# Matmuls that read their moving columns from two halves by turns, in a gated FNet and SwiGLU kernel

## The chip, the cores and the metric

One core of a Trainium2 chip runs the kernel. The time is the device time in microseconds (us) of one execution. Before the change three runs took 709.20, 709.61 and 709.89 us, so the median is 709.61 us. The host transposes and stacks the inputs before the launch and the output after it; that work is not in the time.

## The reference

`x` is 2048 x 512 (sequence by hidden), all data float32. Cut to what matters:

```python
g = sigmoid((x * gate_w).sum(-1, keepdims=True))
a = dft_seq_re @ (x @ dft_hid_re.T) - dft_seq_im @ (x @ dft_hid_im.T)   # real part of a 2-D DFT
b = (silu(x @ w1) * (x @ w3)) @ w2                                       # F = 1376
return g * a + (1 - g) * b
```

## The kernel before, in words

**Layout.** Every product has the sequence position on the free axis: the output is stored as 512 x 2048 (hidden by sequence), and the host transposes it. The sequence is cut into four pieces of `TB = 512` columns, and a matmul on TensorE (PE) takes a 128 x 128 block of weights (the stationary operand) and 128 x 512 moving columns, one such piece, and adds to one PSUM bank of 128 x 512.

**Three matmuls for one.** A float32 number is split into a rounded high part (ScalarE, `high`, line 108) and the rest, a low part (VectorE, `low`, line 111). Both have the type float32r, 4 bytes an element. `mm3` (line 117) multiplies high by high, high by low and low by high, so a product of two blocks is three matmuls. All but the warm-up go through `mm3` (its matmul is line 119) or `half` (line 432), which does the same for the first chunk in another order.

**Seven products for eight.** Blocks are multiplied in a Strassen-like scheme: sums and differences of the four quadrants of each operand (forms such as `T1` to `T4`) give seven products, which are combined after them. VectorE makes the forms (lines 675 and 678 in `sum_c`), ScalarE and VectorE split them, and both read the products from PSUM.

**The stages.** Eleven bfloat16 matmuls on a constant (line 407, into `wps`) warm the engine. The gate stage runs over 21 items, a chunk of 128 hidden units of w1 and w3 with one half of the sequence each, in `gate_up`: x transposed (tile `xo`) is the moving operand, the weights are the stationary one (`wa`, `wb`), the products are X, Y and Z. One spare column of w1 carries `gate_w`, so the gate's score comes out with the last chunk and goes to `gs`. The result h goes to DRAM (`hsp`). Then come eight blocks, in `step`, whose products are called P and whose moving operand is always the tile `zo`:

- F, four blocks, one for each 512 positions: moving is a piece of the sequence DFT matrix (`cc`), stationary is x (`a`, forms A1 and A2). The result is multiplied by g (`gsp`) and goes to `zsp`.
- H, two blocks: moving is h from `hsp`, stationary is w2. The result is multiplied by 1 - g (`ngsp`) and goes to `nbsp`.
- Y, two blocks: moving is `zsp`, stationary is the hidden DFT matrix. The result plus the part in `nbsp` goes to `out`.

So the columns that F or the gate stage leave behind are moving columns once more in Y and H.

**What sets the order.** The order on every engine is written out by hand (`manual_schedule`). A step of the last eight blocks is 12 matmuls on one `zo` tile (6 in a few steps of H). Each step ends in `advance(m)`, which issues the load of what will be wanted 8 steps later (`LEAD + AHEAD`), makes the sums for 4 steps later and splits the `zo` tile for 3 steps later (`LEAD = 3`). There are four `zo` buffers.

**The gate's own work.** `gates` (lines 753 to 762) runs twice, once for each half of the sequence. For each of two pieces of 512 columns VectorE computes 1 - g from g (line 759) into `ng`; then ScalarE negates the second piece of `t` (line 760), and both tiles go to DRAM by GpSimd's queue. The blocks load from there, F from `gsp`, H from `ngsp` (`load_gate`).

Of the kernel before, what the change touches and what calls it, by code (L numbers as in the profile page):

```python
# [10 lines left out]
ALU = mybir.AluOpType  # L11

P = 128
S = 2048
D = 512
F = 1376
KD = D // P
TB = 512
NTB = S // TB
NT = TB // P  # L20
NST = S // P
NG = NST // 2
# [10 lines left out]
def fnet_swiglu_gate_kernel(  # L33
# [20 lines left out]
    nc = tc.nc  # L54
# [25 lines left out]
    def bank(k, name):  # L80
        return psum.tile([P, 512], F32, tag=f"ps{k}", name=name)
# [28 lines left out]
    def low(hi, lo, src):  # L110
        nc.vector.tensor_sub(lo, src, hi.bitcast(F32))  # L111

    def split(hi, lo, src):
        high(hi, src)
        low(hi, lo, src)

    def mm3(ps, ah, al, bh, bl, first, last, chain=False):
        for n, (u, v) in enumerate(((ah, bh), (ah, bl), (al, bh))):
            nc.tensor.matmul(ps, u, v, start=first and n == 0, stop=last and n == 2,  # L119
                             skip_group_check=chain)  # L120


    act0 = const.tile([P, 24], F32, tag="act0", name="act0")
# [139 lines left out]
    def prod(ps, n, wi, xi, start, chain=False):  # L263
        w = WSET[n]
        w, wi = (WA[w], wi) if wi < 3 else (WB[w], wi - 3)
        x = XO[ITEMS[n][1]]
        for q in range(2):
            sl = slice(q * P, (q + 1) * P)
            mm3(ps, w[:, 0, wi, sl], w[:, 1, wi, sl], x[:, 0, xi, q, :], x[:, 1, xi, q, :],
                start and q == 0, q == 1, chain)  # L270
# [148 lines left out]
    C = {(i, j): bank((0, 4, 6, 7)[2 * i + j], f"C{i}{j}") for i in range(2) for j in range(2)}  # L419

    def half(i, j, w, x, start):

        wp = lambda h, sl: a21[:, h, sl] if w is None else WA[0][:, h, w, sl]
        xp = lambda q, h: b12[:, h, q * 512 : (q + 1) * 512] if x is None else XO[0][:, h, x, q, :]
        hh, lh, hl = (0, 0), (1, 0), (0, 1)
        order = [(r, *p) for r in range(2) for p in ((hh, hl, lh) if w is None else (hh, lh, hl))]
        if w == x == 0:
            order = [(r, *p) for some in ((hh, lh), (hl,)) for r in range(2) for p in some]  # L430
        for n, (r, u, v) in enumerate(order):
            nc.tensor.matmul(C[i, j], wp(u, slice(r * P, (r + 1) * P)), xp(r, v),  # L432
                             start=start and n == 0, stop=not start and n == 5)

    def xo_half(k, q):
        i = OPS.index(k)
# [15 lines left out]
    split_by_both(*xo_half("B11", 0))  # L452
    split(*xo_half("B11", 1))
    half(0, 0, 0, 0, True)
    split(a21[:, 0], a21[:, 1], WS[0][:, 3])
    half(1, 0, None, 0, True)
    high(*wa_parts(0, 1, 3)[::2])
    low(*wa_parts(0, 1, 2))
    split_by_both(*xo_half("B21", 0))
    split(*xo_half("B21", 1))  # L460
    low(*wa_parts(0, 2, 3))
    half(0, 0, 1, 1, False)
    split(b12[:, 0], b12[:, 1], ST[0, "B12"])
    half(1, 0, 2, 1, False)
# [120 lines left out]
    for n in range(NI):  # L585
        if n in W2_AT:
            p = W2_AT.index(n)
# [4 lines left out]
        if n in A1_AT:  # L592
            p = A1_AT.index(n)
# [9 lines left out]
    n = NI - 1 - LOOK  # L603
# [149 lines left out]
    def gates(g):  # L753

        t, ng = GATES.pop(g)
        nc.scalar.activation(t, t, AF.Sigmoid)
        for j, (v, w) in enumerate(((-1.0, 1.0), (1.0, -1.0))):
            b = slice(j * 512, (j + 1) * 512)
            nc.vector.tensor_scalar(ng[:, b], t[:, b], v, w, op0=ALU.mult, op1=ALU.add)
        nc.scalar.activation(t[:, 512:], t[:, 512:], AF.Copy, scale=-1.0)  # L760
        nc.gpsimd.dma_start(gsp[g], t)
        nc.gpsimd.dma_start(ngsp[g], ng)
# [101 lines left out]
    def step(m):  # L864
# [19 lines left out]
        for r in range(2):  # L884
            sl = slice(r * P, (r + 1) * P)
            for n, zn in steps:
                for i in range(ni):
                    w = ws[2 * n + i]
                    b = slice(i * 512, (i + 1) * 512)
                    mm3(ps[r], w[:, 0, f, sl], w[:, 1, f, sl], zn[:, 0, b], zn[:, 1, b],  # L890
                        own and n == 0 and i == 0, n == NQ[blk] - 1 and i == ni - 1, not own)
# [55 lines left out]

    at(0, 0, lambda: nc.scalar.activation(act0, act0, AF.Sigmoid))
    at(0, 4, gates, 0)
    at(1, 3, gates, 1)  # L950
    late = [(w2, w2sp, p) for p in range(len(W2_AT), NP2)] + [(dd, dsp, p) for p in range(KD)]
    for i, (src, sp, p) in enumerate(late):
        blk, b = 1 + i // 2, i % 2
        n = (17, 24)[b]
# [84 lines left out]
```

## Time and profile before

| | |
|---|---|
| median of 3 runs | 709.61 us (709.20 to 709.89) |
| span of the profiled execution, first to last instruction | 707.2 us |
| TensorE matmul (PE) busy | 702.7 us, 99%, 3089 matmuls |
| TensorE weight load (PEld) busy | 579.2 us, 82% |
| VectorE (DVE) busy | 605.3 us, 86% |
| ScalarE (ACT) busy | 370.1 us, 52% |
| GpSimd (POOL) busy | 64.2 us, 9% |
| moved by DMA | 172.54 MB, mean 244 GB/s |

The time of the profiled execution is shown by its span alone; 2.4 us lie between the span and the median of the runs. PE busy means that a matmul is in the engine, by ends that are modelled, and matmuls overlap: one takes 389 ns from start to end, and the next starts well before that. The pace of the matmuls is therefore read as a stretch divided by the matmuls in it, not from the duration of one. PEld is the load of the next stationary block, which runs beside the matmul before it.

### The profile page before, as it was taken

What the parts mean: (1) busy time and instruction counts of PE and PEld (TensorE: products, weight loads), DVE (VectorE), ACT (ScalarE), POOL (GpSimd) and SP (SyncE); (2) the same over time, 40 slices, a digit from 0 to 9 for tenths busy, and PEclk for the clock granted to TensorE, in tenths of its full rate; (3) what the DMA queues carried; (4) which work ended last, traced back from release to release, by engine and by line L of the source; (5) the groups of instructions that cost most, each with busy time, mean ns of one, the idle gap of its engine ahead of it and who ended that gap; (6) DMA issues with size and microseconds to landing.
All of it is one profiled execution on the core that took longest, in us unless ns stands there. A gap on an engine that the chain in (4) does not pass through costs nothing.

```text
span 707.2 us, 8607 instructions
## 1 busy us (share of the span) xinstructions
PE 702.7 (99%) x3089; PEld 579.2 (82%) x3089; DVE 605.3 (86%) x737; ACT 370.1 (52%) x480; POOL 64.2 (9%) x118
## 2 busy tenths in 40 slices
PE   9999999999999999999999999999999999999997
PEld 6888888888888888888888888888888888888886
DVE  7989978887679999877999689969997896898985
ACT  6666555655446754454554454544555454455452
POOL 0011111211010000000110001100110000000000
PEclk9999999999999999999999999999999999999999
DMA  7665546589997566712595238914999971873932
GB/s 282 239 261 228 214 181 255 184 320 352 419 410 273 212 208 237 277 60 89 181 388 220 90 131 322 335 59 180 389 418 416 355 272 53 301 286 134 320 120 89
DMA packets 45547, 172.54 MB, mean 244 GB/s; under 512 B 5312, under 2 KB 5696, under 8 KB 41664
## 3 DMA queue, kind: packets, MB, share of 16 engines
q1 hardware_dynamic: 32608, 118.63, 45.7%
q0 software_dynamic: 12608, 52.97, 18.9%
q8 instruction: 24, 0.39, 0.2%
q10 hardware_dynamic: 288, 0.39, 0.2%
q14 instruction: 19, 0.16, 0.1%
HBM read 114.82 MB, written 57.16 MB: 243 GB/s over the span
## 4 chain that ended last, share of the span: by engine, by line
PE 99%; DVE 0%; ACT 0%; issue 0%
PE P L119 69%; PE X L119 16%; PE Z L119 8%; PE Y L119 4%; PE C L432 2%; PE wps L407 1%; DVE zc L829 0%; ACT zc L827 0%
## 5 line engine op out<-in xcount | busy, mean ns | idle before, releaser
L119 PE MATMUL P<-zo,a 128*128 128x512 f32 x1344 | 304.8, 389 | 0.0
L119 PEld LDWEIGHTS P<-zo,a 128*128 128x128 f32 x1344 | 252.3, 188 | 52.4
L108 ACT ACTIVATE zo<-B 128x1024 fp32r<-128x1024 f32 (+1 forms) x182 | 189.6, 1045 | 190.6 <-PE P L119 101.2
L111 DVE TENSOR_TENSOR zo<-B,zo 128x1024 fp32r<-128x1024 f32 (+1 forms) x182 | 218.0, 1204 | 48.7 <-ACT zo L108 48.2
L119 PE MATMUL P<-zo,H 128*128 128x512 f32 x468 | 106.2, 389 | 0.0
L119 PEld LDWEIGHTS P<-zo,H 128*128 128x128 f32 x468 | 87.8, 188 | 18.2
L675 DVE TENSOR_TENSOR B<-B,B 128x1024 f32<-128x1024 f32 (+1 forms) x78 | 92.9, 1191 | 0.1
L119 PE MATMUL X<-xo,wb 128*128 128x512 f32 x378 | 92.7, 389 | 0.0
L119 PEld LDWEIGHTS X<-xo,wb 128*128 128x128 f32 x378 | 70.9, 188 | 14.7
L119 PE MATMUL P<-zo,Y 128*128 128x512 f32 x336 | 76.3, 389 | 0.0
L119 PEld LDWEIGHTS P<-zo,Y 128*128 128x128 f32 x336 | 63.1, 188 | 13.1
L327 POOL DMA_DIRECT2D hsp<-h x42 | 23.1, 550 | 127.3 <-DVE h L381 76.1
L119 PE MATMUL X<-xo,wa 128*128 128x512 f32 x126 | 32.0, 389 | 0.0
L119 PE MATMUL Y<-xo,wa 128*128 128x512 f32 x126 | 32.0, 389 | 0.0
L119 PE MATMUL Z<-xo,wb 128*128 128x512 f32 x126 | 32.0, 389 | 0.0
L119 PE MATMUL Z<-xo,wa 128*128 128x512 f32 x126 | 32.0, 389 | 0.0
L678 DVE TENSOR_TENSOR B<-B,B 128x1024 f32<-128x1024 f32 x26 | 31.7, 1220 | 0.0
L904 ACT ACTIVATE zu<-P 128x512 f32<-128x512 f32 x32 | 19.1, 598 | 20.4 <-PE P L119 20.4
L375 DVE TENSOR_TENSOR u<-u,X 128x512 f32<-128x512 f32 x21 | 14.4, 688 | 16.8 <-PE X L119 16.8
L119 PEld LDWEIGHTS Y<-xo,wa 128*128 128x128 f32 x126 | 23.6, 188 | 4.9
L119 PEld LDWEIGHTS X<-xo,wa 128*128 128x128 f32 x126 | 23.6, 188 | 4.9
L119 PEld LDWEIGHTS Z<-xo,wb 128*128 128x128 f32 x126 | 23.6, 188 | 4.9
(137 smaller groups left out, 552.2 us busy)
## 6 DMA issues: line engine op xcount, KB each, us to landing
B<-cc SPq DMA_DIRECT2D x64, 512.0 KB, 6.3
hsp<-h POOLq DMA_DIRECT2D x42, 256.0 KB, 3.6
B<-hsp SPq DMA_DIRECT2D x20, 512.0 KB, 10.5
wbsp<-wb POOLq DMA_DIRECT2D x8, 1024.0 KB, 4.2
wb<-wbsp SPq DMA_DIRECT2D x8, 1024.0 KB, 7.5
B<-zsp SPq DMA_DIRECT2D x16, 512.0 KB, 8.4
H<-w2sp SPq DMA_DIRECT2D x6, 1024.0 KB, 9.2
ws<-w SPq DMA_DIRECT2D x11, 512.0 KB, 5.2
```

Of the source, the lines that this page charges most:

```text
L108: nc.scalar.activation(hi, src, AF.Copy)
L111: nc.vector.tensor_sub(lo, src, hi.bitcast(F32))
L119: nc.tensor.matmul(ps, u, v, start=first and n == 0, stop=last and n == 2, skip_group_check=chain)
L327: nc.gpsimd.dma_start(hsp[g, b + k, j // 2, :, j % 2 * 512 : (j % 2 + 1) * 512], h)
L375: nc.vector.tensor_add(u4, u4, x)
L407: nc.tensor.matmul(wps, warm[:, :P], warm, start=True, stop=True)
L432: nc.tensor.matmul(C[i, j], wp(u, slice(r * P, (r + 1) * P)), xp(r, v), start=start and n == 0, stop=not start and n == 5)
L675: nc.vector.tensor_add(t, t, RAW[blk, b, q][:, :n])
L678: nc.vector.tensor_sub(t, RAW[blk, "B12", q], t)
L904: nc.scalar.activation(U[name][:, r], ps[r], AF.Copy)
```

## The change

`mm3` and `half` no longer call the matmul directly, but through a helper that reads the 512 moving columns in another order: column 0 of the first half of 256, column 0 of the second half, column 1 of the first, column 1 of the second, and so on. In memory the two columns read one after the other lie 256 elements (1024 bytes) apart. What is written to PSUM is still 512 columns in a row.

So that the results are the same numbers, the host lays out the columns of x transposed and of the sequence DFT matrix in each piece of 512: the even ones first, then the odd ones. Read by turns they come out in their own order, and so the gate stage and F leave their columns in order. H and Y read such columns by turns, so that what they write is in turned order: position a * 256 + n of a piece is column 2n + a. For H's result the gate 1 - g has to be in the same order, and VectorE writes it so (every second element of `ng` from one half of `t`); the host undoes the order of the output. Numbers, sizes and order of the instructions on every engine stay as they were, as do all DMAs, their sizes and the patterns in which they read and write.

```diff
+    def turns(v):
+        return v.rearrange("p (a n) -> p n a", a=2)
+
+    def matmul(ps, u, v, **kw):
+        nc.tensor.matmul(ps.rearrange("p (n a) -> p n a", a=2), u, turns(v), **kw)
+
     def mm3(ps, ah, al, bh, bl, first, last, chain=False):
         for n, (u, v) in enumerate(((ah, bh), (ah, bl), (al, bh))):
-            nc.tensor.matmul(ps, u, v, start=first and n == 0, stop=last and n == 2,
-                             skip_group_check=chain)
+            matmul(ps, u, v, start=first and n == 0, stop=last and n == 2,
+                   skip_group_check=chain)
...
-            nc.tensor.matmul(C[i, j], wp(u, slice(r * P, (r + 1) * P)), xp(r, v),
-                             start=start and n == 0, stop=not start and n == 5)
+            matmul(C[i, j], wp(u, slice(r * P, (r + 1) * P)), xp(r, v),
+                   start=start and n == 0, stop=not start and n == 5)
...
-            nc.vector.tensor_scalar(ng[:, b], t[:, b], v, w, op0=ALU.mult, op1=ALU.add)
+            nc.vector.tensor_scalar(ng[:, b].rearrange("p (n a) -> p a n", a=2),
+                                    t[:, b].rearrange("p (a n) -> p a n", a=2),
+                                    v, w, op0=ALU.mult, op1=ALU.add)
...
+    def turns(v):
+        return v.reshape(*v.shape[:-1], TB // 2, 2).swapaxes(-1, -2).reshape(v.shape)
+
     cq = [
-        a[k].T.reshape(2, NG // 2, 2, P, NTB, TB).transpose(4, 0, 1, 3, 2, 5)
+        turns(a[k].T.reshape(2, NG // 2, 2, P, NTB, TB)).transpose(4, 0, 1, 3, 2, 5)
...
-    xq = x.T.reshape(2, 2, P, 2, 2, TB).transpose(3, 0, 4, 2, 1, 5)
+    xq = turns(x.T.reshape(2, 2, P, 2, 2, TB)).transpose(3, 0, 4, 2, 1, 5)
...
-    return np.ascontiguousarray(r.results[0]["out"].T).reshape(1, S, D)
+    y = r.results[0]["out"].reshape(D, NTB, TB // 2, 2).transpose(1, 3, 2, 0)
+    return np.ascontiguousarray(y).reshape(1, S, D)
```

## The prediction

> **What bounds the kernel now.** I read the page first: busy times, then the chain that ended last.
>
> ```profile
> PE 702.7 (99%) x3089; PEld 579.2 (82%) x3089; DVE 605.3 (86%) x737; ACT 370.1 (52%) x480; POOL 64.2 (9%) x118
> ...
> PE 99%; DVE 0%; ACT 0%; issue 0%
> ```
>
> The matmul engine is 99% of the span and of the chain. Busy time of overlapping matmuls proves no rate, so the next views are PE's waits and the pieces of the chain in order of time.
>
> ```profile
> PE wps L407 <- PEq L1029: 0.8, 1, 0.8
> ```
>
> ```profile
> 213.87 1.36 PE Z L119 x6
> 215.23 1.36 PE X L119 x6
> 216.59 486.89 PE P L119 x2148
> ```
>
> In the whole span the one wait of matmuls is 0.8 us, ahead of the warm-up. From 216.59 us on, 2148 matmuls follow each other in 486.89 us, one every 226.7 ns; 1.36 us for 6 in the gate stage is the same 227 ns. So nothing that feeds PE is ever late, and the time is a count of matmuls by a pace. The count without the warm-up is 3089 - 11 = 3078 (its row is below), and 3078 x 226.7 ns = 697.7 us of the 707.2 us span. The question is whether the order of reading changes 226.7 ns: each nanosecond of it is worth 3.08 us, or 0.43%.
>
> What is the 226.7 ns made of? I asked for the clock, for the weight loads, and for the start of the program, where the same 512 columns are read as bfloat16.
>
> ```profile
> core 0: 707.2 us, clock 0.999
> ```
>
> ```profile
> L407 PE MATMUL wps<-const-bfloat16-1.0 128*128 128x512 bf16 x11 | 4.9, 627 | 0.8 <-PEq L1029 0.8
> ```
>
> ```profile
> 3.29 0.15 PEld L407 LDWEIGHTS <-const-bfloat16-1.0 128*128 128x128 bf16 x1 [0.28 <-issue]
> ...
> 4.57 0.15 PEld L407 LDWEIGHTS <-const-bfloat16-1.0 128*128 128x128 bf16 x1 [0.28 <-issue]
> ```
>
> ```profile
> L432 PEld LDWEIGHTS C<-xo,wa x30: 187/188/303, 5.3 to 16.1; 128*128 128x128 f32 x30
> L432 PE MATMUL C<-xo,wa x30: 388/389/664, 5.3 to 16.3; 128*128 128x512 f32 x30
> ```
>
> ```profile
> L119 PEld LDWEIGHTS P<-zo,a 128*128 128x128 f32 x1344 | 252.3, 188 | 52.4
> ```
>
> The warm-up's loads, one for each matmul, lie 1.28 us / 3 = 427 ns apart, and the first float32r load and matmul still take up to 303 and 664 ns, against 188 and 389 later. I read this as a start at half the later clock; if so, 512 columns need 427 / 2 = 213.3 ns at the later one, an estimate from these rows. The steady pace of 226.7 ns is then 13.3 ns, or 6%, above it. This **excess** isn't the clock (0.999), nor a semaphore (no wait), nor plainly the duration of the weight load (188 ns, with 52.4 us / 1344 = 39 ns of rest behind each). What is left is the fetching of operands or a fixed cost of each float32r matmul. For fetching speaks that the warm-up at the lower rate of 2-byte columns shows no excess over a round 2 x 213.3; against it, that at half the clock an excess might be hidden.
>
> [...]
>
> **The change part by part.** *The reading order, 3078 times.* The trace has no matmul whose moving columns lie apart, so the price is bounded from both sides. Best: the excess lies in fetching neighbours from one place, and two places by turns hide it all, -13.3 ns each, -41.0 us. Worst: a column of float32r comes no faster than at the program's start, one in 427 / 512 = 0.83 ns, and the excess stays: 440 ns, +213.3 x 3078 = +657 us. Between them lies no change at all. I take -10 ns (three quarters of the excess) as the value of the likeliest case, nearest to the steady rows; the rest is a start of each matmul that no order of columns removes. 3078 x 10.0 ns = -30.8 us. That it is the likeliest is a choice between a gain and a loss, made because the excess has no other owner that the trace shows and because each half now has twice the time to deliver its next column.
>
> *What is late next.* PE is covered everywhere now; a pace of 216.7 ns shortens every stretch by 4.4%, while the work of the others stays. The stretches with the least cover:
>
> ```profile
> 220.00:300.00 80.00, 80.00 (x354) 66.24 (x354) 77.27 (x91) 45.83 (x60) 3.21 (x6) 1.00 0.70 252
> 340.00:380.00 40.00, 40.00 (x178) 33.14 (x177) 38.77 (x47) 20.48 (x27) 5.94 (x11) 1.00 0.90 330
> 420.00:460.00 40.00, 40.00 (x178) 33.14 (x177) 38.80 (x45) 19.76 (x23) 5.39 (x10) 1.00 0.87 329
> 500.00:560.00 60.00, 60.00 (x266) 49.71 (x265) 53.16 (x58) 29.16 (x35) 5.63 (x10) 1.00 1.02 415
> ```
>
> The columns are busy us of PE, weight load, VectorE, ScalarE and GpSimd, then clock, DMA share, GB/s. From 220 to 300 us VectorE needs 77.27 us and would have 76.5: 0.8 us short. From 340 and from 420 it needs 38.8 and would have 38.2: 0.6 us short each. The lead of three steps is 3 x 12 x 216.7 ns = 7.8 us, so this is mostly absorbed. From 500 to 560 us the DMA engines are full (1.02) and would have 57.4 us for 60 us of transfers: 2.6 us short, against loads that run 8 steps (21 us) ahead. I give back 2 us for all of it, with bounds of 0 and 4.6 (the sum of the shortfalls).
>
> *The second gate.* Four VectorE instructions write every second element:
>
> ```profile
> L759 DVE TENSOR_SCALAR u2g<-p5g x4: 420/421/422, 230.4 to 300.8; 128x512 f32<-128x512 f32 x4
> ...
>   ACT p5g L760: 2.2, 2
> ```
>
> They take 4 x 0.42 = 1.7 us. No row shows one with scattered writes: between nothing and twice as long, +0.84 us at each of two places. Queued behind them are VectorE's next sums, and ScalarE's line 760 waits for them (2.2 us for both). All of this stands behind the lead of 7.8 us; I take 0, and 1.7 us if that cover were gone.
>
> *Nothing else moves.* No instruction is added, removed or moved on any queue. The weight loads, splits, sums, PSUM reads and DMAs are the same contiguous ones, and the host's layouts cost no device time.
>
> **The sum**, against the profiled execution: 707.2 - 30.8 + 2.0 + 0 = 678.4 us of span, with the 2.4 us around it **680.8 us** (709.6 is 2.4 above that span, too).
>
> **The rivals.** About 0.2%, 1.4 us, is what a measurement of this kernel can tell from no change.
>
> *A. The order is free.* The excess is a fixed cost of a float32r matmul (a swap of weights, say), and a column costs the same from wherever it comes. For it: the pace is 226.7 ns in every stage, whatever the tiles and however busy the other engines are. Against it: nothing. 709.6 us, with at most 1.7 us for the gate: chance 0.18.
>
> *C. Jumps add to the excess.* If the excess is the price of going from one spot of memory to the next, and neighbours share a spot, columns by turns pay it more often. Twice the excess is a pace of 240.0 ns, 3078 x 13.3 = +41.0 us, 750.6 us; four times it is 266.7 ns, +123 us, 832.7 us. For it: the same excess that the forecast needs; against it: two spots at a time may both be held. It decides as soon as the pace is above 226.7 ns, since PE has nothing to hide behind. Chance 0.20.
>
> *B. Half rate.* This is the rival on the other side in full: each column is a fetch of its own, and fetches come at the rate of the start, 427 ns for 512. Place: every matmul; VectorE, ScalarE and DMA would then idle for nearly half the time. Without the excess 426.7 ns, +200 x 3078 = +616 us, 1325 us; with it 440 ns, 1366 us. It decides once the moving side gives less than 512 columns in 226.7 ns, 2.26 a nanosecond; in order it gives that, and no row shows what it gives out of order. Chance 0.20.
>
> [...]
>
> **How the numbers follow.** The forecast has 0.42, with its own range from 668.6 (all of the excess gone, nothing given back) to 704 us (an eighth of it gone). A has 0.18, C 0.20, B 0.20. Cases of both signs hold much of the chance: 0.42 faster, 0.18 the same, 0.40 slower. The range over the forecast, A and C, from 668 to 835 us, leaves out B, 2 in 10; beyond it a miss would be near 1325 to 1366.
>
> **What would show it.** In the profile after, the long piece of the chain, P with some 2148 matmuls, gives the pace at once: 465 us for the forecast, 487 for A, 515 to 573 for C, 917 or more for B. In the forecast PE would show its first waits for VectorE's `zo` splits or DMA between 220 and 560 us, 5 us at most in all; in B and C it has none and VectorE's share of the span falls from 86%. Line 759 shows the price of scattered writes. The forecast is wrong in its main step if the matmuls keep 226.7 ns or take more; it is wrong in the smaller one if the pace falls but waits return more than 4.6 us.

## The result

The changed kernel takes 679.73 us (median of 4 runs, 679.20 to 680.68) against 709.68 us for the kernel before (median of 4). The ratio is 0.958, with a 95% interval from 0.9566 to 0.9593. The forecast was 680.8 us.

From the page of the profile after, the span, the busy times and the shares of the engines in the chain that ended last:

```profile
span 678.0 us, 8627 instructions
...
PE 671.2 (99%) x3089; PEld 581.8 (86%) x3089; DVE 602.1 (89%) x737; ACT 366.9 (54%) x480; POOL 64.0 (9%) x118
...
PE 51%; issue 37%; DMA 6%; DVE 3%; POOL 3%; ACT 0%; SPq 0%; POOLq 0%; DVEq 0%; ACTq 0%
```

The engines' counts of work are the same (the 20 instructions more than before, 8627 instead of 8607, are semaphore instructions on ScalarE and TensorE); the matmuls hold PE 31.5 us less. The chain no longer runs on PE alone: from a late matmul it goes back to VectorE and to the transfers that fed it. "Issue" in it is time without a releaser that the profile shows; only the piece after the last wait is unbroken. That piece is the pace, in the view of the chain's pieces:

```profile
508.24 165.83 PE P L122 x767
```

165.83 us / 767 is 216.2 ns. The piece begins behind a wait and ends with a matmul's tail; in the trace the steady starts lie 215 to 217 ns apart, 215.8 in the mean. Before it was 226.7, so 10.8 of the 13.3 ns that the prediction called the excess are gone. Next the waits of PE, then those of its weight loads:

```profile
PE P L122 <- DVE zo L111: 1.0, 2, 0.7
PE wps L414 <- PEq L1042: 0.8, 1, 0.8
PE C L122 <- ACT xo L108: 0.6, 1, 0.6
PE X L122 <- DVE xo L111: 0.2, 1, 0.2
```

```profile
PEld P L122 <- DVE zo L111: 2.5, 4, 1.1
PEld C L122 <- ACT xo L108: 1.3, 2, 1.1
...
PEld X L122 <- DVE xo L111: 0.6, 1, 0.6
```

Before, the only wait of matmuls was the one ahead of the warm-up. Now four more, 1.8 us in all, stand behind ScalarE's and VectorE's splits, and where a load waits its matmul is late as well (near 253 us both start at 253.42 us). The busy times by stretch show the longest of them near 250 us:

```profile
245.00:260.00 15.00, 13.96 (x64) 11.46 (x63) 14.93 (x20) 8.47 (x11) 0.00 (x0) 1.00 0.70 225
260.00:500.00 240.00, 240.00 (x1114) 210.18 (x1113) 219.83 (x243) 122.64 (x145) 21.51 (x40) 1.00 0.61 225
```

Behind the window and its length, the first number is PE's: 13.96 of 15 us, while VectorE (the third) is busy for 14.93. From 260 to 500 us PE is covered throughout, with 1114 matmuls. Before the change VectorE was full in the first of the two windows as well, but PE was covered:

```profile
245.00:260.00 15.00, 15.00 (x68) 12.43 (x67) 15.00 (x23) 9.81 (x17) 0.00 (x0) 1.00 0.49 163
```

VectorE's four instructions for the second gate now take 476 instead of 421 ns:

```profile
L766 DVE TENSOR_SCALAR u2g<-p5g x4: 459/476/484, 222.2 to 290.6; 128x512 f32<-128x512 f32 x4
```

The order that they write is that of H and Y: position 2n + a of a piece is column a * 256 + n. The description of the change has it the other way round, which is the host's layout of the inputs.

### The profile page after: what moved, and what is told of

Read it like the earlier page. It is cut to its first block, busy times and chain, and to the rows that moved or that the text cites. A ratio compares the mean times of both kernels' runs of the same rounds, so it can differ in the third digit from the quotient of the medians.

```text
span 678.0 us, 8627 instructions
## 1 busy us (share of the span) xinstructions
PE 671.2 (99%) x3089; PEld 581.8 (86%) x3089; DVE 602.1 (89%) x737; ACT 366.9 (54%) x480; POOL 64.0 (9%) x118
## 4 chain that ended last, share of the span: by engine, by line
PE 51%; issue 37%; DMA 6%; DVE 3%; POOL 3%; ACT 0%; SPq 0%; POOLq 0%; DVEq 0%; ACTq 0%
PE P L122 24%; PE X L122 15%; PE Z L122 8%; PE Y L122 3%; DMA B<-hsp 2%; DMA dsp<-late_0l 2%; DMA xs_B<-xt 1%; POOL zsp L821 1%; DMA p5g<-gs 1%; POOL dsp L803 1%; POOL w2sp L803 1%; DVE wa L111 1%; DVE xs_B L214 1%; DVE zo L111 0%; DVE xo L111 0%
## 5 line engine op out<-in xcount | busy, mean ns | idle before, releaser
L122 PE MATMUL P<-zo,a 128*128 128x512 f32 x1344 | 290.9, 379 | 1.0 <-DVE zo L111 1.0
L122 PE MATMUL P<-zo,H 128*128 128x512 f32 x468 | 101.4, 379 | 0.1
L122 PE MATMUL X<-xo,wb 128*128 128x512 f32 x378 | 89.2, 380 | 0.2 <-DVE xo L111 0.2
L122 PE MATMUL P<-zo,Y 128*128 128x512 f32 x336 | 72.7, 379 | 0.0
L122 PE MATMUL Y<-xo,wa 128*128 128x512 f32 x126 | 30.6, 379 | 0.0
L122 PE MATMUL Z<-xo,wb 128*128 128x512 f32 x126 | 30.6, 379 | 0.0
L122 PE MATMUL Z<-xo,wa 128*128 128x512 f32 x126 | 30.6, 379 | 0.0
L111 DVE TENSOR_TENSOR wa<-ws,wa 128x768 fp32r<-128x768 f32 (+1 forms) x22 | 19.3, 880 | 9.6 <-ACT wa L108 9.5
```

The lines of the kernel that those rows point to most:

```text
L122: nc.tensor.matmul(ps.rearrange("p (n a) -> p n a", a=2), u, turns(v), **kw)
```

## The experiments

Two questions were open: what in the new order frees the matmuls, and what the excess was. The experiments e1 to e6 and e11 change only the order in which the moving columns are read; e7 and e9 cut each matmul in two; e8 and e10 change the reading of the weights; e12 moves sums to another engine. All but e12 were run once, with a profile; beside them the kernel before took 709.0 to 709.5 us. A *line* is here a name for four neighbouring columns, 16 bytes; where the memory itself has such borders no run shows.

**e1, pairs inside one line of four columns.**

```diff
-        nc.tensor.matmul(ps.rearrange("p (n a) -> p n a", a=2), u, turns(v), **kw)
+        v = v.rearrange("p (m a n) -> p m n a", a=2, n=2)
+        nc.tensor.matmul(ps.rearrange("p (m n a) -> p m n a", a=2, n=2), u, v, **kw)
```

The experiments up to e6 and e11 differ in the first line with a plus (and the second in step with it, so that PSUM is written in a row as before).

> The changed kernel, with another order of reading: in every four neighbouring columns 0, 2, 1, 3, so that the step inside a pair is 2 elements (8 bytes) and all four lie within 16 bytes. Only the order of the columns differs, so the output's columns and the second gate no longer match. Theory of places (neighbours in time must come from two places that lie apart): as in order, 226.7 ns a matmul, 707 us of span. Rival, the step (an innermost step of 1 is what costs the excess, any other step is free of it): 215.8 ns, 678 us. Rival, a fixed cost that a one-level pattern has: 215.8 ns as well.

Its long piece of the chain:

```profile
217.05 486.89 PE P L119 x2148
```

486.89 us, to the digit what the kernel before has: 226.7 ns, and 709.41 us. So neither the step of 2 nor the pattern of several levels helped by itself; both rivals fall.

**e2, two lines side by side.**

```diff
+        v = v.rearrange("p (m a n) -> p m n a", a=2, n=4)
```

> The changed kernel, reading by turns from two runs of four columns that lie side by side (0, 4, 1, 5, 2, 6, 3, 7, then the next eight), 16 bytes apart instead of 1024. Output columns and second gate don't match. Theory of places, if 16 bytes are enough to be another place: 215.8 ns a matmul, 678 us of span; if the distance has to be larger: 226.7 ns, 707 us. Rival, the step: 215.8 ns.

```profile
508.02 165.83 PE P L119 x767
```

The same piece as in the changed kernel, and 679.55 us. Two places 16 bytes apart are enough for 215.8 ns. e1 and e2 differ in that alone: whether the two columns of a turn lie 8 bytes apart, inside one line, or 16, in two.

**e3, every fourth column.**

```diff
+        v = v.rearrange("p (a n) -> p n a", a=128)
```

> The changed kernel, reading every fourth column (0, 4, 8, ... 508, then 1, 5, ...): each column lies 16 bytes from the one before, and a spot is come back to only 128 columns later. Output columns and second gate don't match. [...] Rival, the step: 215.8 ns.

```profile
434.66 990.96 PE P L119 x2148
```

990.96 / 2148 = 461.3 ns, 1431.12 us: twice the time. The theory that any change of place helps is wrong; in e2 a line is used up within 8 columns, here only after 128 columns does the next read of it come. So the loss of the prediction's rival B is there in this order, and dearer (461.3 ns) than its 427 to 440 ns.

**e4, long runs by turns.**

```diff
+        v = v.rearrange("p (a n b) -> p n a b", a=2, b=128)
```

> The changed kernel, reading the two halves by turns in runs of 128 columns (first quarter, third, second, fourth): a pattern of three levels, but inside a run the columns are neighbours. Output columns and second gate don't match. Theory of places and the rival of the step: 226.7 ns a matmul, 707 us (within 1 ns, for three jumps a matmul). Rival, a fixed cost that only a one-level pattern has: 215.8 ns, 678 us.

```profile
216.92 486.89 PE P L119 x2148
```

709.28 us, and the same 486.89 us for 2148 matmuls as in order. The theory's number came, and the last rival falls: turns after 128 columns change nothing.

**e5 and e6, four and sixteen places by turns.** The edits are `a=4` and `a=16` for `a=2` in the changed kernel.

> The changed kernel, reading by turns from four quarters (0, 128, 256, 384, 1, 129, ...), 512 bytes apart. Output columns and second gate don't match. Theory (what costs is a run of columns within 16 bytes, and a few such lines are held between reads): 215.8 ns a matmul, 678 us, if at least four lines are held. Rival (only two are held): between 226.7 and 461 ns, the pace that the step of 4 had.

> The changed kernel, reading by turns from sixteen runs of 32 columns (0, 32, 64, ... 480, 1, 33, ...), 128 bytes apart, so a line is come back to 16 columns later. Output columns and second gate don't match. Theory with few held lines: 461 ns a matmul as with the step of 4, 1430 us. Rival (any line is held until all four columns are read, up to 16): 215.8 ns, 678 us.

The long pieces of e5, then e6:

```profile
269.62 608.61 PE P L119 x2148
```

```profile
410.31 934.39 PE P L119 x2148
```

That is 283.3 and 435.0 ns, 883.71 and 1350.18 us. So for e5 the rival came, for e6 the theory, 6% below its 461. Four lines at a time are already 31% dearer than two (283.3 / 215.8), and sixteen cost nearly as much as coming back only after 128 columns. Two is the one number of places tried that gains.

**e7, matmuls of 256 columns in order.**

```diff
-        nc.tensor.matmul(ps.rearrange("p (n a) -> p n a", a=2), u, turns(v), **kw)
+        for i in range(2):
+            b = slice(i * 256, (i + 1) * 256)
+            nc.tensor.matmul(ps[:, b], u, v[:, b], start=start and i == 0, ...)
```

> Each matmul of 512 columns is cut into two of 256, read in order as before the change; weights are loaded for both; output columns and second gate don't match. If the excess grows with the columns (10.8 ns for 512): two of 106.7 + 2.5 + 5.4 = 114.6 ns, 229 ns for 512, about 715 us. If it is a fixed cost of each matmul or each weight load: two of 120.0 ns, 240 ns for 512, about 748 us. If the weight load becomes the bound, more than that: up to its 188 ns for each.

```profile
229.27 515.53 PE P L120 x4296
```

515.53 / 4296 = 120.0 ns, 750.40 us. From 512 to 256 columns a matmul falls by 106.7 ns, which is the 256 columns alone, and the whole 13.3 ns stay. So the excess comes once for each matmul and its weight load, not with the columns, as the second case had it. By itself this looks like the fixed cost of rival A; but a fixed cost can't depend on the order of the columns, as it does in e1 and e2. What else comes once for each matmul is the load of the next weights, which runs beside it (6167 of each in this run, loads busy for 99% of the span and matmuls for 99%). Whether it is the owner is the question of e8 to e10.

**e8, the kernel before with weights at a step of 2.**

```diff
-            sl = slice(q * P, (q + 1) * P)
+            sl = slice(q, q + 2 * P - 1, 2)
```

The same is done at the other two places where the stationary columns are chosen.

> The kernel before the change, with the weights of each matmul read with a step of 2 (every second of 256 columns) instead of 128 neighbours; the moving columns are read in order. Rows of the products change places, so the output doesn't match. Theory (the excess belongs to the moving columns alone): 226.7 ns a matmul, 707 us. Rival (the excess is moving reads that the weight load's reads push aside, one for each 16 bytes of weights, 32 lines in a load of 128 columns): twice as many lines, an excess up to twice as large, about 237.5 ns, 741 us.

```profile
222.98 501.21 PE P L119 x2148
```

501.21 / 2148 = 233.3 ns, 729.66 us. The moving columns are read as before, yet each matmul is 6.7 ns slower: the way in which the weights are read changes the pace. The excess over 215.8 ns goes from 10.8 to 17.5 ns, less than double; the theory that it lay with the moving columns alone falls, and the rival's size was too large (237.5).

**e9, 256 columns by turns.** As e7, with `rearrange("p (a n) -> p n a", a=2)` on each 256 columns.

> As the cut into two matmuls of 256 columns, but each of the two is read by turns from its own two halves of 128. Output columns and second gate don't match. Theory (the excess of 10.8 ns is moving reads held up by the reads of the next weights, and reading by turns between two lines leaves room for these): 106.7 + 2.5 = 109.2 ns each, 218.4 for 512, about 685 us, with more waits for VectorE; the second sign would be that 120.0 in order falls by the same 10.8 ns as 226.7 did. Rival (a fixed swap of weights that turning hides only behind 512 columns, or a load that lasts longer than 109 ns): still near 120 ns each, 748 us.

```profile
213.81 479.73 PE P L120 x4296
```

111.7 ns, 699.12 us: 8.3 ns less than in order, not the 10.8 expected, and nothing like the rival's 120. Where a weight load falls to every 256 columns, 2.5 ns over the expected 109.2 remain. In e7, where one comes every 120 ns, a load lasts 192 ns from start to end.

**e10, the changed kernel with weights at a step of 2.** The edit of e8 on the changed kernel.

> The changed kernel with the weights of each matmul read with a step of 2, as was done to the kernel before. Rows of the products change places, so the output doesn't match. Theory (reading by turns leaves room for the weights' reads): the step, which cost 6 ns a matmul in order, costs nothing or nearly so, 215.8 to 217 ns, 678 to 682 us. Rival (turning only shifts the collision by luck of this pattern of weights): the same 6 ns or more come back, 222 ns or above, 697 us.

```profile
508.42 165.83 PE P L122 x767
```

679.92 us, and the piece is that of the changed kernel. The same edit that costs 6.7 ns a matmul in order costs nothing by turns. The loads themselves do last longer with the step than the 188 ns of before, but as much in e8 (the first row) as here (the second):

```profile
L119 PEld LDWEIGHTS P<-zo,a 128*128 128x128 f32 x1344 | 263.4, 196 | 50.2
L122 PEld LDWEIGHTS P<-zo,a 128*128 128x128 f32 x1344 | 263.3, 196 | 28.5 <-DVE zo L111 2.0
```

So the load's length does not set the pace either. e8 and e10 together carry the explanation: the loss depends on how both streams are read, the weights and the columns, and turning takes it away. What is measured are four paces (226.7 and 233.3 in order, 215.8 and 215.8 by turns). That the reads of the two get in each other's way is the author's reading of them; no view shows single reads.

**e11, two columns of each line, then the next line.**

```diff
+        v = v.rearrange("p (m a b) -> p a m b", a=2, b=2)
```

> The changed kernel, reading two neighbours of every four columns (0, 1, 4, 5, 8, 9, ... then 2, 3, 6, 7, ...): each line of four is hit twice in a row and left. Output columns and second gate don't match. [...] Theory of collisions: 256 line reads instead of 128 leave less room beside the weights' reads, so more than the 226.7 ns of in order, 230 to 285 ns (the four places gave 283.3), 717 to 885 us.

```profile
427.49 973.77 PE P L119 x2148
```

453.3 ns and 1406.73 us, as dear as one hit a line. The expectation failed. Two columns of a line in a row did not help; what the orders at 215.8 and 226.7 ns share is that all four columns of a line are read within 4 or 8 columns. 453.3 is twice 226.7, for twice as many visits to lines (256 instead of 128 a matmul); but e3's 512 visits take only 461.3, so a price for each visit doesn't fit. Why pairs cost as much as single columns stays open.

**e12, an attempt to remove waits that are left.**

```diff
-        nc.vector.tensor_sub(r[:, :256], r[:, 256:512], r[:, :256])
+        nc.gpsimd.tensor_sub(r[:, :256], r[:, 256:512], r[:, :256])
```

> The changed kernel, with the eight small sums ahead of the second forms of x (128 x 256 each, 0.42 us on VectorE, 230 to 250 us) on GpSimd. The reference's result. Theory (the waits left in the changed kernel, 1.5 us near 250 us among them, are VectorE being full there): those waits go, the time falls by 1 to 1.5 us, 0.2%, to about 678.4 us. Rival (GpSimd is slower at them, or holds VectorE up where both read): no change or up to 2 us more.

The rows are the sums on GpSimd, from the tile's view, and the waits of PE:

```profile
L174 POOL TENSOR_TENSOR xs<-xs x8: 1147/1709/11462, 225.0 to 243.8; 128x256 f32<-128x256 f32 x8
```

```profile
PE P L122 <- DVE zo L111: 2.3, 3, 1.3
```

The theory fails and its rival came: 681.60 us in 5 runs, a ratio of 0.9615 to the kernel before (0.9602 to 0.9628), above the changed kernel's whole interval. A sum takes 1.15 to 11.46 us on GpSimd instead of 0.42, and the wait for `zo` grows from 1.0 to 2.3 us. No version tried beats the changed kernel by more than a measurement can tell; e2, at 679.55 us, is level with it.

## Why the prediction was right

*The bound.* A count by a pace: 3078 matmuls, and nothing else in the way. That held, but for the 4.1 us of new waits below; every run above is read by it.

*The excess, and what it belongs to.* The prediction split 226.7 ns into 213.3 and 13.3 and left two owners, fetching or a fixed cost. The 213.3 was an estimate, half of the warm-up's 427 ns. The granted clock is 1.00 from 2 to 5 us as well, so a lower clock is not what the trace shows; a halved pace it does show: after the change the starts of the last warm-up matmuls, from 4.06 us on, lie 220 and 218 ns apart. And e7's 106.7 ns for 256 columns make 213.4 for 512. That the warm-up has no excess over 2 x 213.3 says nothing, since 213.3 was taken from it. The excess has something of both: e7 shows that it comes once a matmul (13.3 ns with 256 columns as with 512), e2 that it yields to the order of the columns (215.8 ns), e8 and e10 that it depends on the step of the weights, in order (233.3 ns) and not by turns (215.8). The prediction let the weight load go because it ends 39 ns early. Its duration was indeed not the matter (196 ns in e8 and in e10, at 233.3 and 215.8 ns a matmul); the order in which it takes the weights was. The reason given for the gain, that each half has twice the time for its next column, is not what the runs show: a price of columns would halve with 256 of them, and e7's 13.3 ns are whole; nor need the second place be another half (e2). So the forecast chose the right owner, fetching, and the right direction, for a reason that was in part wrong.

*The size.* -10.0 ns was taken, three quarters of the excess by choice and not from a row, and -10.8 measured; that it came so near is in part luck. So the term is -33.3 us (3078 x 10.83) instead of -30.8. What remains over 213.3 is 2.5 ns; that this rest is a start of each matmul, as the prediction took its 3.3 ns to be, no run shows.

*What was late next.* Taken 2.0 us, with 4.6 as the bound. The spans differ by 29.2 us (707.2 to 678.0), so 33.3 - 29.2 = 4.1 us came back. The starts of the matmuls in the trace show where: 1.6 us from 245 to 262 us, where VectorE was shortest of time, 0.4 us at 508 us, 1.6 us in the gate stage (near 30 and 180 us), and the rest in the opening (C behind ScalarE's split) and behind the last matmul. So the stretches that the prediction named gave back 2.0 us, as taken, though with other shares: 1.6 us for the 0.8 at 220 to 300 us, nothing at 340 to 460, 0.4 us for the 2.6 at 500 to 560. The gate stage, which it left out, brought nearly as much again: from 26 to 32 us VectorE is busy for 5.97 of 6 us, and from 176 to 184 us the DMA share is 1.02. That all of it together stays under the bound is luck. A long wait also costs more than itself: the late matmul's own weight load starts only with it (both at 253.42 us), and the next start comes 320 ns later instead of 216, seven times in the trace from 28 us on. The two misses, 2.5 us too little gain and 2.1 us too little given back, nearly cancel, so the span came 0.4 us below the 678.4 of the sum; the other 0.7 us of the 1.1 is that 1.7 us lie around this span, not 2.4.

*The second gate.* Between nothing and twice as long: it was 13% (421 to 476 ns), 0.2 us in all.

*The rivals.* A would have been right if turning could not reach the cost: e7's fixed 13.3 ns is what spoke for it. C and B lost for two places only. With four places C's largest price (266.7 ns) is passed at 283.3, and with sixteen, or a step of 4, B's 427 to 440 ns is there with 435 and 461. The prediction had no row that told two places from four, so that the change turns between two is luck as far as its rows go; that its case of 0.42 came true does not show the reasoning to be stronger than that.

*What stays open.* How the two streams share the memory inside was not seen; that turning leaves room between reads of lines is the author's reading, which fits e1, e2, e8, e9 and e10, but e11 does not follow from it. Every matmul here has a weight load (3089 of each), so no run shows whether one without a load has any excess in order; a cost of starting a matmul that depends on how both operands are read would look the same.

## What to carry to other kernels

Here float32r matmuls of 512 columns, each with a weight load, ran back to back at 226.7 ns, with no wait and a clock of 0.999, and 4.8% of the pace (4.2% of the time) was had without moving an instruction. Where a kernel looks the same, try that: read the moving columns by turns from two 16-byte lines, and lay the data out so that the result fits. Interleave two (215.8 ns), neither four (283.3) nor sixteen (435.0), and use each line up within 8 columns, as e2 does (with 128 columns between reads of a line, e3 took 461.3). A pace that is exact and the same in every stage still has parts; changing one stream of reads at a time shows which.

## What the runs showed of the hardware

- With its 512 columns in order, a float32r matmul beside the load of the next 128 weight columns takes 10.8 ns more than by turns (226.7 against 215.8), though that load ends 39 ns before the next one begins; with the weights at a step of 2 it is 17.5 ns more (233.3), and by turns the step costs nothing (215.8).
- Moving columns of 4 bytes, ns for 512: one line at a time 226.7; two lines by turns 215.8; four 283.3; sixteen 435.0; a new line at each column 461.3; two columns of each line 453.3.
- A VectorE instruction on 512 float32 columns that writes every second element took 476 instead of 421 ns.
